# The third tile's x loaded ahead of the second half of the key weights, two copies moved between engines, one normalisation put later

## The chip, the cores and the metric

One core of a Trainium2 chip runs the whole program. The metric is the device time of one execution in microseconds; less is better. The kernel before takes 1095.43 us, the median of three runs (1094.91 to 1096.3).

## The reference, cut to what matters

x is 2048 tokens of 576 features. A gate g = sigmoid(x · gate_w) mixes a linear-attention block and a channel MLP:

```python
q, k, v = split(x @ wqkv)                    # 32 heads of 18
pq, pk  = phi(q), phi(k)                     # phi(t) = where(t > 0, t + 1, exp(t)) + 1e-6
kv, z   = einsum(pk, v), pk.sum(tokens)      # per head
a = ((pq @ kv) / (pq . z + 1e-6)) @ wo
b = gelu(layernorm(x) @ w1 + b1) @ w2 + b2   # w1: 576 x 4608, w2: 4608 x 576
out = g * a + (1 - g) * b
```

## The kernel before, in words

Work on tokens goes by tiles of 128, sixteen in all, in the order of a list ORDER; `first` is its first three (called tile 0, 1 and 2 below). Every matrix is multiplied in float32 by splitting both factors into a high part (float32r, what TensorE multiplies at speed) and a low part (the rest), and by summing high·high, low·high and high·low. A split is thus always two steps: a copy that rounds to the high part, and a subtraction on VectorE (DVE) that gives the low part. Nearly everything is recorded through a small helper (line 120), so that profile lines read L120 and are told apart by the names of their tiles.

Each engine does its instructions in the order in which the program writes them; nothing reorders them. The second half of the program (the MLP) is written in an order that a planner computes; the change does not touch it.

Names at the start. `t` is the raw x of a tile, loaded transposed in three DMAs on the queue of SyncE (SP): the main part from `in_xm` (256 KB) and two from `in_xe` (32 KB each). `s` is a raw half of a weight matrix: the main part from `in_wm` (576 KB) and two from `in_we` (72 KB each). There are four halves: KEY 0, KEY 1, QUERY 0, QUERY 1. The main part of KEY 0 comes in three pieces on ScalarE's (ACT's) queue. `y` holds the split x and the split weights. `split_x` and `split_w` make them: the copy on ACT, the low part on DVE. KEY 1 is 128x1450 (two more columns per row block than QUERY 0's 128x1440, for the sums that the gate and the layer norm need).

`first_keys(n, half)` is 14 matmuls of TensorE (PE): tile n times a half of the key weights. Its order takes the high·high products first, then low x · high weights, and those with the weights' low part from the tenth on. `both_phi(n)` applies phi to both halves of tile n's keys: for each half two instructions on ACT (`e<-ps`, `e<-e`) and one on DVE (`k<-ps,e`), then two short ones for the sums of x (`gsum`, `nmean`). The tile `e` has two buffers, so that the third `e<-ps` waits until DVE has read the first. `first_queries(n, half)` are the same 14 matmuls with the query weights; their results alternate between two PSUM banks, 6 and 7, so that tile 2's may only start when phi of tile 0's has been read from bank 6 by DVE (`accs<-ps,e`).

Loads: every DMA that SP or ACT issues takes the next of eight semaphores in turn, and waits until the DMA eight places earlier has landed (the `DMAHW` waits below).

Some 190 us later the attention's output matrix is made. `project_values(t)`, t = 0 to 4, computes one of five row blocks of `wp` on PE (12 matmuls; 6 for the last) into one of two pairs of PSUM banks in turn (banks 6 and 7 for t = 0, 2, 4; banks 4 and 5 for t = 1, 3); ACT copies the high part out (`wp<-ps`), DVE subtracts for the low part (`wp<-ps,wp`), and then the pair is free. `normalize(i, (1,))` multiplies tile i's phi(q) by its reciprocal denominator on DVE (`accs<-accs,den`); `tail_q(i)` copies its last 64 columns on ACT (`tail<-accs`). `transpose_q(i)` turns tile i on PE (`ps<-accs`, `ps<-accs,tail`) and splits it (`qt`). Between `transpose_q(0)` and `transpose_q(1)` PE projects the last tile's queries (28 matmuls, `ps<-y`) into banks 4 and 5.

Of the kernel before, what the change touches and what calls it, by code (L numbers as in the profile page):

```python
# [11 lines left out]
AF = mybir.ActivationFunctionType  # L12
# [81 lines left out]
def raw(ap):  # L94
    return ap.bitcast(F32)


def halves(ap):
    return ap.rearrange("p (a n) -> p a n", a=2)


def heads(ap):
    return ap.rearrange("p (h d) -> p h d", d=DH)


def half_cols(half):
    return slice(half * HALF, (half + 1) * HALF)
# [19 lines left out]
def tile_gated_mix(ctx: ExitStack, tc: tile.TileContext, x, xm, xe, wm, we, wvm, wve, wo, um, ue, w2, b1, b2, gw, out):  # L127
    nc = tc.nc
    pe, act, dve, pool = (InOrder(tc, e) for e in (nc.tensor, nc.scalar, nc.vector, nc.gpsimd))
# [9 lines left out]
    def two_of(ring):  # L139
        n = next(ring)  # L140
        return ps[:, n:n + 2]
# [4 lines left out]
    def load_twice(dst, src, by=sp):  # L146
        for half in range(2):
            by.dma_start(dst[half * 64:(half + 1) * 64], src)
# [48 lines left out]
    QUERY, KEY = range(2)  # L197
# [25 lines left out]
    def load_w(part, half, pieces=((0, 5),), by=sp):  # L223
        if (part, half) not in wraw:
            wraw[part, half] = wsp.tile([P, 5, HALF + 2], F32, name="s", tag="s")
        s = wraw[part, half]
        main = wm[part * 2 + half].rearrange("p (t n) -> p t n", t=4)
        tail = we[part * 2 + half]
        for t0, t1 in pieces:
            if t0 < 4:  # L230
                by.dma_start(s[:, t0:min(t1, 4), :HALF], main[:, t0:min(t1, 4)])
            if t1 == 5:
                load_twice(s[:, 4, :HALF], tail, by)

    def split_w(part, half, by=dve, pieces=((0, 5),)):
        w = W[part, half]
        s = wraw[part, half][:, :, :w.shape[2]]
        for t0, t1 in pieces:
            act.activation(w[:, t0:t1], s[:, t0:t1], AF.Copy)
            by.tensor_tensor(out=w[:, 5 + t0:5 + t1], in0=s[:, t0:t1], in1=raw(w[:, t0:t1]), op=OP.subtract)  # L240

    def load_x(i):
        xraw[i] = yt.tile([P, 5, P], F32, name="t")
        sp.dma_start(xraw[i][:, 0:4], xm[i].rearrange("p (t n) -> p t n", t=4))
        load_twice(xraw[i][:, 4], xe[i])

    def split_x(i, pieces=((0, 5),)):
        if i not in xs:
            xs[i] = x_places[PLACE[i] % X_RING]
        to, src = xs[i], xraw[i]  # L250
        for t0, t1 in pieces:
            act.activation(to[:, t0:t1], src[:, t0:t1], AF.Copy)
            if t0 < 4:
                dve.tensor_sub(to[:, 5:9], src[:, 0:4], raw(to[:, 0:4]))
            if t1 == 5:
                dve.scalar_tensor_tensor(to[:, 4], raw(to[:, 4]), low_half[:, 0:1], src[:, 4], op0=OP.mult, op1=OP.add)
# [12 lines left out]
    def project(i, part, half, order=BY_ROWS, n=None, between={}):  # L269
        w = W[part, half]  # L270
        p = banks[i, part, half] = ps[:, next(halves_in) if n is None else n]
        for m, (a, b) in enumerate(order):
            pe.matmul(p[:, :w.shape[2]], xs[i][:, a, :], w[:, b], start=(m == 0), stop=(m == len(order) - 1))
            if m in between:
                between[m]()
# [16 lines left out]
    def keys_phi(i, half):  # L292
        if half == 0:
            K[i] = kp.tile([P, D], F32, name="k")
        phi(K[i], i, KEY, half, (lambda: None, lambda: sums_of_x(i))[half])
# [152 lines left out]
    def load_y(sup, m):  # L448
# [3 lines left out]
    first = ORDER[:FIRST]  # L452
# [5 lines left out]
    act.activation(tiny, ones[:, 0:1], AF.Exp)  # L458
    load_w(KEY, 0, ((4, 5),), act)
    load_x(first[1])  # L460
    load_w(KEY, 1)
    load_x(first[2])
    load_w(QUERY, 0)
    load_xn(first[0])
    load_w(QUERY, 1)
# [4 lines left out]
                       base=0, channel_multiplier=1)  # L470
    pool.affine_select(blocks, blocks, pattern=[[DH, 7], [0, DH]], compare_op=OP.is_ge, fill=0.0,
                       base=DH - 1, channel_multiplier=-1)
    split_x(first[0], ((0, 4),))
    split_w(KEY, 0, pieces=((0, 1), (1, 2)))
    split_x(first[0], ((4, 5),))
    split_w(KEY, 0, pieces=((2, 4), (4, 5)))

    def first_keys(n, half, between={}):
        project(first[n], KEY, half, HI_FIRST, 3 * half + n, between)
# [4 lines left out]
    def both_phi(n):  # L484
        for half in range(2):
            keys_phi(first[n], half)
# [12 lines left out]

    first_keys(0, 0, {0: lambda: warm(1), 1: lambda: warm(1), 2: lambda: warm(1), 3: turn_gate})  # L500
    split_x(first[1])
    first_keys(1, 0)
    dve.tensor_copy(wraw[KEY, 1][:, :, HALF:HALF + 1], column[:, :, None])
    dve.memset(wraw[KEY, 1][:, :, HALF + 1:HALF + 2], 1.0)
    split_w(KEY, 1)
    split_x(first[2])
    load_x(ORDER[3])
    first_keys(0, 1)
    first_keys(1, 1)
    both_phi(0)  # L510
    split_w(QUERY, 0)
    first_keys(2, 0)
    first_keys(2, 1)
    both_phi(1)
    keys_split(first[0])
# [82 lines left out]
    for n in range(FIRST, NT):  # L598
        i, before = ORDER[n], ORDER[n - 1]
# [72 lines left out]
    def normalize(i, parts=(0, 1)):  # L672
        if 0 in parts:
            dens[i] = small.tile([P, H], F32, name="den")
        den = dens[i]
        if 0 in parts:
            dve.tensor_reduce(out=den, in_=heads(qz[i]), op=OP.add, axis=AX.X)
            dve.tensor_tensor(out=den, in0=den, in1=den0, op=OP.add)
            dve.reciprocal(den, den)
        if 1 in parts:  # L680
            dve.scalar_tensor_tensor(heads(acc[i]), heads(acc[i]), EPS_PHI, den[:, :, None].to_broadcast([P, H, DH]),
                                     op0=OP.add, op1=OP.mult)

    def tail_q(i):
        tails[i] = small.tile([P, P], F32, name="tail")
        act.activation(halves(tails[i]), acc[i][:, None, 4 * P:D].to_broadcast([P, 2, 64]), AF.Copy)
# [56 lines left out]
    def project_values(t):  # L743

        pw = two_of(w_pairs)
        own = [(n, j) for n, (to, j) in enumerate(PIECES) if to == t]
        for half in range(2):
            parts = [(kv_parts[a][:, n], wo_parts[b][:, j]) for a, b in TERMS for n, j in own]
            for m, (a, b) in enumerate(parts):
                pe.matmul(pw[:, half, :HALF], a, b[:, half_cols(half)], start=m == 0, stop=m == len(parts) - 1)  # L750
        p = pw[:, :, :HALF]
        act.activation(halves(wp[:, t]), p, AF.Copy)
        dve.tensor_tensor(out=halves(wp[:, 5 + t]), in0=p, in1=halves(raw(wp[:, t])), op=OP.subtract)
# [19 lines left out]
    normalize(1, (0,))  # L773
    project_values(1)
    project_values(2)
    normalize(1, (1,))
    tail_q(1)
    project_values(3)
    project_values(4)
    normalize(2, (0,))  # L780
    transpose_q(0)
    normalize(2, (1,))
# [861 lines left out]
```

## Time and profile before

| | |
|---|---|
| median of three runs | 1095.43 us (1094.91 to 1096.3) |
| the profiled execution, its time | 1096.17 us |
| the profiled execution, its span | 1094.5 us |
| PE busy | 1086.3 us, 99% of the span |
| DVE, ACT, POOL busy | 922.4, 691.3, 236.2 us |
| granted PE clock | full in all forty slices |

PE is the matmuls, PEld the weight loads that overlap them; SPq is SP's queue, that is the instructions that issue DMAs. In a timeline a row is: start in us, duration in us, engine, line, operation, what it writes <- what it reads, shape, how many; in brackets the idle time before it and what ended it. In the chain of waits (the work that ended last, followed back from the end) a row is: start, duration, what.

### The profile page before, as it was taken

Reading aid. Unit: us, or ns where it says so; the run is one execution under the profiler, and the core shown is the slowest. Engines: PE = TensorE matmul, PEld = TensorE weight load, DVE = VectorE, ACT = ScalarE, POOL = GpSimd, SP = SyncE. Lnnn points to the kernel's source line nnn. Section 1 sums busy time; section 2 is a strip of 40 time slices with the busy share of each in tenths; the row PEclk is TensorE's granted clock in tenths of the full one; section 3 lists DMA queues with packets and bytes.
Section 4 is the critical chain, followed back from the end, with each engine's and each line's share of the span. In section 5 each row is a group of like instructions: output and inputs, shape, how many; then the busy total and the mean of one; then the engine's idle time right before and its main releaser. Section 6 shows DMA issues by size and latency. Waiting matters only on the chain.

```text
span 1094.5 us, 18650 instructions
## 1 busy us (share of the span) xinstructions
PE 1086.3 (99%) x6712; PEld 996.6 (91%) x6712; DVE 922.4 (84%) x1558; ACT 691.3 (63%) x1235; POOL 236.2 (22%) x232
## 2 busy tenths in 40 slices
PE   9999999999999999999999999999999999999998
PEld 8999999999898889988889988989899999999898
DVE  4568786896799999899999997988887888878888
ACT  6677766454667887777877876455555555455552
POOL 2111113431123232332111202121122211221110
PEclk9999999999999999999999999999999999999999
DMA  6466772745745665764556559574444445444432
GB/s 179 135 87 190 172 218 101 278 178 191 249 156 188 196 203 185 239 209 169 194 184 220 191 197 396 170 252 118 135 148 118 130 119 148 131 122 118 133 102 87
DMA packets 109006, 189.72 MB, mean 173 GB/s; under 512 B 8940, under 2 KB 68604, under 8 KB 104818
## 3 DMA queue, kind: packets, MB, share of 16 engines
q1 hardware_dynamic: 108002, 187.78, 53.7%
q8 instruction: 53, 0.87, 0.3%
q10 hardware_dynamic: 720, 0.74, 0.2%
q14 instruction: 39, 0.32, 0.1%
q0 software_dynamic: 192, 0.01, 0.0%
HBM read 121.70 MB, written 66.80 MB: 172 GB/s over the span
## 4 chain that ended last, share of the span: by engine, by line
PE 92%; DVE 3%; DMA 3%; ACT 1%; issue 0%; SPq 0%; ACTq 0%; DVEq 0%
PE ps L120 92%; DVE accs L120 1%; DMA accs<-moments 1%; DMA yd<-ystage 1%; DMA s<-in_wm 0%; DVE h L120 0%; DMA ystage<-late_acc 0%; DMA fresh<-in_ue 0%; DMA s<-in_we 0%; DVE wa L120 0%; DVE region L120 0%; DVE ystage L120 0%; DVE wb L120 0%; DVE fresh L120 0%; ACT u L120 0%
## 5 line engine op out<-in xcount | busy, mean ns | idle before, releaser
L120 PEld LDWEIGHTS ps<-region,h 128*128 128x128 f32 x3072 | 437.5, 188 | 30.2 <-ACT ps L120 4.7
L120 PE MATMUL ps<-region,h 128*128 128x288 f32 x3072 | 456.8, 295 | 0.8 <-DVE accs L120 0.7
L120 DVE TENSOR_TENSOR accs<-ps,accs 128x576 f32<-128x576 f32 x330 | 246.1, 753 | 60.7 <-PE ps L120 53.9
L120 PE MATMUL ps<-y,wa 128*128 128x512 f32 x1008 | 257.6, 392 | 0.0
L120 PEld LDWEIGHTS ps<-y,wa 128*128 128x128 f32 x1008 | 180.8, 188 | 30.5 <-ACT ps L120 0.2
L120 POOL TENSOR_TENSOR fresh<-fresh 128x288 f32<-128x288 f32 (+1 forms) x128 | 117.1, 918 | 409.5 <-DVE accs L120 144.5
L120 PE MATMUL ps<-y,wb 128*128 128x512 f32 x756 | 199.2, 393 | 0.4 <-ACT u L120 0.4
L120 DVE TENSOR_TENSOR h<-u,h 128x512 fp32r<-128x512 f32 x240 | 165.4, 702 | 8.7 <-ACT u L120 8.7
L120 PEld LDWEIGHTS ps<-y,wb 128*128 128x128 f32 x756 | 133.8, 188 | 21.1 <-ACT u L120 0.6
L120 PE MATMUL ps<-y 128*128 128x288 f32 (+2 forms) x950 | 133.9, 297 | 2.2 <-DVE wp L120 1.1
L120 PEld LDWEIGHTS ps<-y 128*128 128x128 f32 (+1 forms) x950 | 129.8, 188 | 4.4 <-DVE wp L120 1.8
L120 ACT ACTIVATE region<-fresh 128x576 fp32r<-128x576 f32 (+1 forms) x132 | 81.2, 625 | 73.9 <-PE ps L120 73.3
L120 ACT ACTIVATE ps<-ps 128x576 f32<-128x576 f32 (+1 forms) x127 | 78.6, 621 | 45.0 <-PE ps L120 21.5
L120 POOL TENSOR_TENSOR u<-u 128x512 f32<-128x512 f32 x44 | 57.1, 1298 | 193.2 <-DVE h L120 54.8
L120 DVE TENSOR_TENSOR region<-fresh,region 128x576 fp32r<-128x576 f32 (+1 forms) x132 | 94.3, 727 | 1.1 <-ACT region L120 1.1
L120 ACT ACTIVATE u<-ps 128x512 f32<-128x512 f32 x73 | 43.0, 589 | 68.2 <-PE ps L120 68.2
L120 ACT ACTIVATE h<-u 128x512 fp32r<-128x512 f32 x128 | 73.4, 621 | 9.9 <-DVE u L120 5.5
L120 ACT ACTIVATE h<-u,b1s 128x512 fp32r<-128x512 f32 x73 | 52.6, 722 | 42.2 <-DVE u L120 42.1
L120 PE MATMUL ps<-wp,qt 128*128 128x288 f32 x448 | 63.0, 297 | 0.0
L120 DVE TENSOR_TENSOR u<-ps,u 128x512 f32<-128x512 f32 x74 | 50.4, 683 | 13.6 <-PE ps L120 12.7
L120 PEld LDWEIGHTS ps<-wp,qt 128*128 128x128 f32 x448 | 59.8, 188 | 0.0
L120 DVE TENSOR_TENSOR u<-u 128x512 f32<-128x512 f32 x84 | 58.0, 691 | 1.7 <-POOL u L120 1.1
(139 smaller groups left out, 1044.8 us busy)
## 6 DMA issues: line engine op xcount, KB each, us to landing
w1d<-wa SPq DMA_DIRECT2D x17, 1280.0 KB
wa<-w1d SPq DMA_DIRECT2D x68, 320.0 KB
fresh<-in_w SPq DMA_DIRECT2D x70, 288.0 KB
y<-yd SPq DMA_DIRECT2D x14, 1280.0 KB
w1d<-wb SPq DMA_DIRECT2D x17, 960.0 KB
wb<-w1d SPq DMA_DIRECT2D x51, 320.0 KB
yd<-ystage SPq DMA_DIRECT2D x28, 320.0 KB
fresh<-in_um SPq DMA_DIRECT2D x64, 128.0 KB
```

Of the source, the lines that this page charges most:

```text
L120: self.last = self.tc.keep_in_program_order(op(*args, **kwargs))
```

## The change

Three edits at two places.

1. At the start SP issues the three loads of tile 2's x ahead of those of KEY 1. To go with it, tile 2's x is split, and multiplied with KEY 0, before KEY 1 is split; and QUERY 0 is split before phi of tile 0's keys.
2. The high part of tile 0's x (its main part, 128x512) is copied by DVE and no longer by ACT.
3. Around 200 us, `normalize(1, (1,))` moves behind `project_values(3)`, and `tail_q(1)` behind `project_values(4)`.

```diff
-    def split_x(i, pieces=((0, 5),)):
+    def split_x(i, pieces=((0, 5),), on_dve=False):
...
-            act.activation(to[:, t0:t1], src[:, t0:t1], AF.Copy)
+            if on_dve:
+                dve.tensor_copy(to[:, t0:t1], src[:, t0:t1])
+            else:
+                act.activation(to[:, t0:t1], src[:, t0:t1], AF.Copy)
...
     load_x(first[1])
+    load_x(first[2])
     load_w(KEY, 1)
-    load_x(first[2])
     load_w(QUERY, 0)
...
-    split_x(first[0], ((0, 4),))
+    split_x(first[0], ((0, 4),), on_dve=True)
...
     first_keys(1, 0)
+    split_x(first[2])
+    first_keys(2, 0)
     dve.tensor_copy(wraw[KEY, 1][:, :, HALF:HALF + 1], column[:, :, None])
     dve.memset(wraw[KEY, 1][:, :, HALF + 1:HALF + 2], 1.0)
     split_w(KEY, 1)
-    split_x(first[2])
     load_x(ORDER[3])
     first_keys(0, 1)
     first_keys(1, 1)
+    split_w(QUERY, 0)
     both_phi(0)
-    split_w(QUERY, 0)
-    first_keys(2, 0)
     first_keys(2, 1)
...
     project_values(1)
     project_values(2)
+    project_values(3)
     normalize(1, (1,))
+    project_values(4)
     tail_q(1)
-    project_values(3)
-    project_values(4)
     normalize(2, (0,))
```

SP's queue at the start, before (-) and after (+); the rows ahead of these are tile 0's and tile 1's x:

```order
-L120 DMA s<-in_wm 128x4x288 [waits DMAHW2_49]
-L120 DMA s<-in_we 64x288 [waits DMAHW4_49]
-L120 DMA s<-in_we 64x288 [waits DMAHW5_49]
-L120 DMA t<-in_xm 128x512 [waits DMAHW6_49]
-L120 DMA t<-in_xe 64x128 [waits DMAHW7_49]
-L120 DMA t<-in_xe 64x128 [waits DMAHW0_49]
+L120 DMA t<-in_xm 128x512 [waits DMAHW2_49]
+L120 DMA t<-in_xe 64x128 [waits DMAHW4_49]
+L120 DMA t<-in_xe 64x128 [waits DMAHW5_49]
+L120 DMA s<-in_wm 128x4x288 [waits DMAHW6_49]
+L120 DMA s<-in_we 64x288 [waits DMAHW7_49]
+L120 DMA s<-in_we 64x288 [waits DMAHW0_49]
```

The six loads have changed places three by three; each place keeps its semaphore, so KEY 1's main load now stands in the place that waits for `DMAHW6`, tile 1's main part.

ACT at the start, before (-) and after (+): 128x640 is a tile's x, 128x1450 is KEY 1, 128x1440 is QUERY 0, `e` is phi of keys.

```order
-L120 ACTIVATE y<-s 128x1450 [waits DMAHW4_49,DMAHW5_49,DMAHW2_49,DVE_49]
-L120 ACTIVATE y<-t 128x640 [waits DMAHW7_49,DMAHW6_49,DMAHW0_49]
-L120 ACTIVATE e<-ps 128x288 [waits PE_49]
-L120 ACTIVATE e<-e 128x288 [waits Activation_49]
-L120 ACTIVATE e<-ps 128x288 [waits PE_49]
-L120 ACTIVATE e<-e 128x288 [waits Activation_49]
-L120 ACTIVATE gsum<-ps 128x1
-L120 ACTIVATE nmean<-ps 128x1
+L120 ACTIVATE y<-t 128x640 [waits DMAHW5_49,DMAHW4_49,DMAHW2_49]
+L120 ACTIVATE y<-s 128x1450 [waits DMAHW6_49,DMAHW7_49,DMAHW0_49,DVE_49]
 L120 ACTIVATE y<-s 128x1440 [waits DMAHW3_49,DMAHW2_49,DMAHW1_49]
```

Tile 2's x now goes ahead of KEY 1, and the six instructions of phi of tile 0, which stood between KEY 1 and QUERY 0, stand behind QUERY 0 (their added rows follow directly).

DVE around 200 us, before (-) and after (+): `wp` is a row block's low part, `accs<-accs,den` the normalisation of tile 1.

```order
 L120 RECIPROCAL den<-den 128x32 [waits DVE_49]
-L120 TENSOR_TENSOR wp<-ps,wp 128x576 [waits Activation_49] x2
+L120 TENSOR_TENSOR wp<-ps,wp 128x576 [waits Activation_49] x3
 L120 SCALAR_TENSOR_TENSOR accs<-accs,den 128x576 [waits DVE_49]
-L120 TENSOR_TENSOR wp<-ps,wp 128x576 [waits Activation_49] x2
+L120 TENSOR_TENSOR wp<-ps,wp 128x576 [waits Activation_49]
 L120 TENSOR_REDUCE den<-qz 128x32 [waits Pool_49]
```

The fourth row block's low part now stands ahead of the normalisation. On ACT, likewise, the copies of the fourth and fifth row blocks stand ahead of `tail<-accs`, which waits for that normalisation.

## Prediction

> **What bounds the kernel now.** I read the page first, then the chain of waits whole, at the start and around 200 us, and then the timelines of the engines there.
>
> ```profile
> span 1094.5 us, 18650 instructions
> PE 1086.3 (99%) x6712; PEld 996.6 (91%) x6712; DVE 922.4 (84%) x1558; ACT 691.3 (63%) x1235; POOL 236.2 (22%) x232
> ...
> 14.48 182.82 PE ps L120 x1229
> 201.67 320.14 PE ps L120 x1996
> ```
>
> PE is idle for 1094.5 - 1086.3 = 8.2 us in all, and the chain is PE alone from 14.48 to 197.30 and from 201.67 to 521.8. So whatever PE gains or loses at the two places of the change is kept, one for one, and no more than a few microseconds are to be had. A measurement of this kernel tells about 0.2%, 2.2 us, from no change.
>
> The two breaks of the chain are where the change works. The first, as the chain has it:
>
> ```profile
> 1.74 4.98 DMA s<-in_wm
> ...
> 7.25 3.94 DMA s<-in_we
> ...
> 11.30 1.43 ACT y L120
> ...
> 12.75 1.68 DVE y L120
> ```
>
> KEY 1's last small load, issued at 7.25, lands at 11.19; ACT copies the high parts from 11.30, DVE makes the low parts from 12.75, and PE goes on at 14.48. The second:
>
> ```profile
> 197.32 0.66 ACT wp L120
> ...
> 198.01 0.76 DVE wp L120
> 198.76 1.19 DVE accs L120
> ...
> 199.98 0.31 ACT tail L120
> 200.29 0.55 ACT wp L120
> ...
> 200.86 0.77 DVE wp L120
> ```
>
> The fourth row block's copy (ACT 200.29, DVE 200.86) stands behind the third's, the normalisation and the tail, and PE waits for it until 201.67.
>
> **Part 3, around 200 us.** PE's weight loads:
>
> ```profile
> 195.43 1.62 PEld L120 LDWEIGHTS ps<-y 126*128 126x128 f32 x12 [0.17 <-DVE wp L120]
> 197.31 2.43 PEld L120 LDWEIGHTS ps<-y 126*128 126x128 f32 x18 [0.26 <-DVE wp L120]
> 201.67 3.75 PEld L120 LDWEIGHTS ps<-y 128*128 128x128 f32 x28 [1.38 <-DVE wp L120]
> ```
>
> The third row block begins at 195.43 and ACT copies it at 197.32, 1.89 later; the fourth begins at 197.31, so its copy can start at 199.20, if nothing stands ahead of it. After the change nothing does. DVE follows 0.69 after ACT (197.32 to 198.01), takes 0.76, and PE hears 0.04 later (200.86 + 0.77 to 201.67): 200.69 instead of 201.67, a gain of 0.98 of the 1.38 us idle. The bounds are narrow: the 28 matmuls can't start before the transposes of tile 0 end, so the gain is at most 1.38, and at least nothing. What moves back: the normalisation ends near 202 instead of 199.95. Its next reader is the transposition of tile 1, which PE reaches at 200.69 + 3.75 = 204.4, more than 2 us later. The tail's copy, now ahead of tile 0's `qt` on ACT, pushes that by less than 1 us, and PE reads `qt` only behind the transposition of tile 1. The fifth row block's low part goes behind the normalisation and stays near 202, where it was. Taken: -0.98.
>
> **Part 2, tile 0's copy on DVE.**
>
> ```profile
> 6.01 0.69 DVE L120 TENSOR_TENSOR y<-t,y 128x512 fp32r<-128x512 f32 x1 [4.62 <-ACT y L120]
> 6.75 0.67 ACT L120 ACTIVATE y<-s 128x576 fp32r<-128x576 f32 x1
> ```
>
> The trace has no such copy on DVE; the subtraction of the same shape, 0.69, bounds it above, 0 below. ACT is freed of one copy, but its third weight piece can't start earlier than 6.72 (1.74 + 4.98 in the chain above, the landing) and starts at 6.75 now. PE reaches that piece's products at the same time, and anyway waits at 12.77 for KEY 1 (below). Taken: 0, hidden by the load; were that cover gone, it would gain at most the 0.7 of a copy.
>
> **Part 1, the loads.** Two quantities decide: A, when ACT starts on KEY 1 (11.30 before), and S, when it starts on QUERY 0 (16.34 before). SP's queue now:
>
> ```profile
> 4.69 0.74 SPq L120 DMA_DIRECT2D s<-in_wm  x1
> 6.73 1.12 SPq L120 DMA_DIRECT2D s<-in_we  x2
> 7.90 0.58 SPq L120 DMA_DIRECT2D t<-in_xm  x1
> 8.52 1.11 SPq L120 DMA_DIRECT2D t<-in_xe  x2
> 9.68 0.60 SPq L120 DMA_DIRECT2D s<-in_wm  x1
> ```
>
> The first two rows are KEY 1, the next two tile 2's x, the last QUERY 0's main load. SP waited until 6.73 for a semaphore of KEY 0, so the places stay when the loads are swapped: KEY 1's main load moves from 4.69 to 7.90, its small loads from 6.73 to 8.52, the last one of them from 7.25 to about 9.07. That load took 3.94 from issue to landing; at 9.07 it lands at 13.0, and A is 13.1.
>
> ```profile
> core 0: us, PE busy (x) PEld busy (x) DVE busy (x) ACT busy (x) POOL busy (x), PEclk, DMA share, GB/s
> 12.00:14.00 2.00, 1.24 (x10) 1.23 (x9) 1.25 (x1) 1.97 (x4) 0.00 (x0) 1.00 1.03 292
> 14.00:16.20 2.20, 1.97 (x15) 1.73 (x15) 1.65 (x4) 0.84 (x3) 0.00 (x0) 1.00 1.05 368
> ```
>
> Bounds for A: tile 2's 320 KB at 368 GB/s put in front is 0.9, so 12.2 at best; QUERY 0, main load issued at 9.68 and ACT at it at 16.34, took 6.66, so 7.90 + 6.66 = 14.6 at worst. I take 13.1. For S: the same bytes lie ahead of QUERY 0 as before and its issue keeps its place, so 16.3 stays the value; best is 12.2 plus its 720 KB at 368 GB/s, 14.2, and worst 14.6 plus 720 KB at 292 GB/s, 17.1.
>
> PE has 14 more matmuls (tile 2 with KEY 0) to do while it waits:
>
> ```profile
> 8.56 3.45 PE L120 MATMUL ps<-y 128*128 128x288 f32 x24
> 12.77 1.24 PEld L120 LDWEIGHTS ps<-y 128*128 128x128 f32 x9 [0.99 <-ACT y L120]
> 14.47 11.91 PEld L120 LDWEIGHTS ps<-y 128*128 128x128 f32 x89 [0.47 <-DVE y L120]
> ```
>
> A matmul takes 11.91 / 89 = 0.134. The 89 are five of tile 0's keys and six groups of 14, of which tile 2's first queries are the last; they thus start at 14.47 + 75 x 0.134 = 24.5. After, PE goes on 3.18 after A (11.30 to 14.48, the same chain of ACT and DVE) with 61 left: A + 3.18 + 8.16 = A + 11.34. At A = 13.1 that is 24.44: the 1.87 us of filled waiting and the 1.8 us of later weights cancel.
>
> But ACT's order has changed, and there the change has its price. Phi of tile 0, done while QUERY 0 was on its way, now stands behind QUERY 0's copy, and with it the whole row of phis up to that of tile 0's queries, whose bank tile 2's queries need:
>
> ```profile
> 16.34 1.41 ACT L120 ACTIVATE y<-s 128x1440 fp32r<-128x1440 f32 x1
> 17.64 0.41 ACT L120 ACTIVATE e<-ps 128x288 f32<-128x288 f32 x1
> 18.43 0.39 ACT L120 ACTIVATE e<-ps 128x288 f32<-128x288 f32 x1
> 19.31 0.78 ACT L120 ACTIVATE ks<-k,eps 128x576 fp32r<-128x576 f32 x1
> 19.98 0.41 ACT L120 ACTIVATE e<-ps 128x288 f32<-128x288 f32 x1
> ...
> 22.94 0.41 ACT L120 ACTIVATE e<-ps 128x288 f32<-128x288 f32 x1 [0.86 <-PE ps L120]
> ...
> 17.78 1.66 DVE L120 TENSOR_TENSOR y<-s,y 128x1440 fp32r<-128x1440 f32 x1 [0.84 <-ACT y L120]
> 19.36 0.81 DVE L120 SCALAR_TENSOR_TENSOR k<-ps,e 128x288 f32<-128x288 f32 x2
> 23.86 0.46 DVE L120 SCALAR_TENSOR_TENSOR accs<-ps,e 128x288 f32<-128x288 f32 x1 [1.29 <-ACT e L120]
> ```
>
> From these rows, counted from S: DVE is through QUERY 0's low parts and starts tile 0's first `k` at S + 3.02 (16.34 to 19.36), and 0.46 later the buffer of `e` is free for tile 1 (S + 3.5; two halves of tile 0 on ACT are done by then). Tile 1: 0.79 for a half (17.64 to 18.43) and 0.88 for a half with its sums (18.43 to 19.31); `ks` 0.67 (19.31 to 19.98); tile 2: 0.79 + 0.88; then tile 0's queries, 0.92 on ACT until DVE starts (22.94 to 23.86) and 0.46 there: S + 3.5 + 1.67 + 0.67 + 1.67 + 1.38 = S + 8.9. Before, this chain ended at 24.32, barely ahead of PE's 24.5. Now tile 2's queries start at the later of A + 11.34 and S + 8.9; with 13.1 and 16.3 that is 25.2, a loss of 0.7. It ends between 23.5 (A 12.2, S 14.2), a gain of 1.0, and 26.0 (A 14.6, S 17.1), a loss of 1.5. Nothing behind gives it back: PE isn't idle again until 200 us.
>
> **Sum.** -0.98 + 0 + 0.7 = -0.25 us on the profiled execution's 1096.17, 1095.9. That execution was 0.7 above the median of the runs, 1095.43; so the median I forecast is 1095.2.
>
> **The rivals.** First, the loads run at their bounds: KEY 1 and QUERY 0, now one behind the other with no small x loads between them, move at the 368 GB/s of the fullest stretch, A = 12.2 and S = 14.2. Then both places gain, 0.98 + 0.97, and the time is 1093.5. Against it: the DMA queue needed until 16.34 for QUERY 0 at 292 to 368 GB/s. The Trainium skill, DMA: Bandwidth & Descriptors, section "Anatomy of one DMA", gives a load some 2 us plus its bytes at 436 GB/s. By that KEY 1 would be there at about 11.3 and QUERY 0 at about 13.4, and the time 1092.7; the same rule puts KEY 1's last small load of before at 9.4, where the trace has 11.19, so here it is queueing that counts. Chance 0.18 for this rival, 0.03 of it for the page's value.
>
> Second, slower: QUERY 0 lands late and ACT, which now holds all phis behind that one wait, stalls. The place is ACT's copy of 128x1440; each microsecond of S beyond 15.6 costs one. From S = 16.6 on, the loss exceeds the gain at 200 us; at S = 17.1 the time is 1096.0; beyond 0.2% it would be only from S = 18.8. For it: SP leaves the DMA queue short between 7.5 and 9, as now only two loads of 32 KB are issued there ahead of KEY 1. Chance 0.17, of which 0.04 beyond 0.2%.
>
> Third, part 3 gives nothing, if PE there waits for something else just as late. Against it: the chain runs through these instructions and no other. Time 1096.1; chance 0.04.
>
> **How the numbers follow.** My own case (A 12.6 to 13.9, S 15.4 to 16.6) has 0.61. The low end of the range, 1093.5, is the first rival's; the high end, 1096.9, is the start's worst case (1.5) with nothing gained at 200 us. Faster by over 0.2% (under 1093.2) needs the page's figures or a lucky median: 0.06; slower by over 0.2% (over 1097.6): 0.05; the rest, 0.89, is within 0.2%.
>
> **What would show it.** In the new profile: KEY 1's copy on ACT (128x1450) near 13.1 and QUERY 0's (128x1440) near 16.3 with ACT idle in front of it; PE idle near 25 ahead of 14 matmuls, released by DVE `accs`; PE's weight loads around 200 idle for some 0.4 instead of 1.38. I am wrong if QUERY 0 is there by 15.6, so that ACT's order costs nothing, or if something outside these 25 us moves.

## The result, and the profile after

The changed kernel takes 1096.87 us, the median of 14 runs (1095.7 to 1098.72), against 1095.45 us for the kernel before on the same chip (14 runs, 1094.34 to 1096.3). The ratio is 1.0016, 95% interval 1.0009 to 1.0023. It is slower by 1.4 us, where I forecast 0.25 us faster. The page has the same picture as before, PE at 99%:

```profile
span 1095.1 us, 18651 instructions
PE 1085.7 (99%) x6712; PEld 995.2 (91%) x6712; DVE 924.3 (84%) x1559; ACT 690.9 (63%) x1234; POOL 235.5 (22%) x232
```

The profiled execution took 1096.82 us, 0.65 more than the one of before; but the latter was 0.7 above its median, so the two traces show only half of the difference of the medians.

The chain of waits of the changed kernel, 0 to 33 us (start, duration, what), answers to the first break of the chain before:

```profile
9.17 4.03 DMA s<-in_we
...
13.28 1.42 ACT y L120
...
14.73 1.68 DVE y L120
...
16.45 8.46 PE ps L120 x61
24.91 0.40 ACT e L120
...
25.34 0.45 ACT e L120
...
25.81 0.47 DVE accs L120
...
26.33 6.69 PE ps L120 x39
```

KEY 1 is copied at 13.28 (forecast 13.1), PE goes on 3.17 later as worked out, and does its 61 matmuls. Then it waits, as forecast, for DVE's `accs`, the release of bank 6. (The chain puts PE ahead of ACT's 24.91, as the 61 matmuls end just then; an experiment below tells whether ACT waited for them.) But tile 2's queries start at 26.33, not at 25.2. PE's weight loads say the same, with the idle time in brackets; the last two rows are `wp`'s third row block and the 28 matmuls behind the fourth:

```profile
14.74 1.24 PEld L120 LDWEIGHTS ps<-y 128*128 128x128 f32 x9 [1.14 <-ACT y L120]
16.45 8.21 PEld L120 LDWEIGHTS ps<-y 128*128 128x128 f32 x61 [0.46 <-DVE y L120]
26.32 1.76 PEld L120 LDWEIGHTS ps<-y 128*128 128x128 f32 x13 [1.67 <-DVE accs L120]
...
197.60 1.61 PEld L120 LDWEIGHTS ps<-y 126*128 126x128 f32 x12 [0.16 <-DVE wp L120]
...
202.89 3.74 PEld L120 LDWEIGHTS ps<-y 128*128 128x128 f32 x28 [0.43 <-DVE wp L120]
```

The start lost 1.8 us; at 197.60 PE is 2.17 behind (195.43 before). Then it is idle for 0.43 instead of 1.38, 0.95 less. Where the missing 1.1 us of the start is lost is seen in the timelines of ACT, DVE and POOL of the changed kernel:

```profile
16.23 1.41 ACT L120 ACTIVATE y<-s 128x1440 fp32r<-128x1440 f32 x1 [1.54 <-DMA s<-in_we]
...
22.21 2.00 DVE L120 SCALAR_TENSOR_TENSOR ks<-k,ks 128x576 fp32r<-128x576 f32 x1 [0.21 <-ACT ks L120]
24.34 0.82 DVE L120 SCALAR_TENSOR_TENSOR k<-ps,e 128x288 f32<-128x288 f32 x2
25.81 0.46 DVE L120 SCALAR_TENSOR_TENSOR accs<-ps,e 128x288 f32<-128x288 f32 x1 [0.65 <-ACT e L120]
...
22.16 1.44 POOL L120 TENSOR_TENSOR pks<-pks,k 128x576 f32<-128x576 f32 x1 [1.37 <-DVE k L120]
```

and of the same two instructions before:

```profile
20.12 0.76 DVE L120 SCALAR_TENSOR_TENSOR ks<-k,ks 128x576 fp32r<-128x576 f32 x1
...
20.33 1.84 POOL L120 TENSOR_TENSOR pks<-pks,k 128x576 f32<-128x576 f32 x1 [2.66 <-DVE k L120]
```

`ks` is the low part of tile 0's phi(k), `pks` the running sum of phi(k) on GpSimd (POOL). Before, DVE began `ks` at 20.12, 0.2 ahead of GpSimd's sum: `ks` took 0.76, and the sum was long (1.84). After, phi of tile 1 is ready before ACT has made the high part of `ks`; GpSimd's sum begins at 22.16, 0.05 ahead of `ks`: the sum takes 1.44, and `ks` 2.00. It ends at 24.21, 0.61 after the sum (22.16 + 1.44 = 23.60). Behind it on DVE stand tile 2's `k` (24.34), which free `e` for ACT's phi of tile 0's queries (24.91), which frees bank 6.

What I could have seen: asked for this tile as a whole, the trace of before gives the spread of all its sixteen `ks` (durations in ns, least, median, most).

```profile
L120 DVE SCALAR_TENSOR_TENSOR ks<-k,ks x16: 749/1238/1348, 20.1 to 172.9; 128x576 fp32r<-128x576 f32 x16
```

The 0.76 us that I carried over was nearly the shortest of them, and the 2.00 of the changed kernel is longer than any.

### The profile page after: what moved, and what is told of

Same layout as the page of the kernel before. It is cut to its first block, busy times and chain, and to the rows that moved or that the text cites. A ratio compares the mean times of both kernels' runs of the same rounds, so it can differ in the third digit from the quotient of the medians.

```text
span 1095.1 us, 18651 instructions
## 1 busy us (share of the span) xinstructions
PE 1085.7 (99%) x6712; PEld 995.2 (91%) x6712; DVE 924.3 (84%) x1559; ACT 690.9 (63%) x1234; POOL 235.5 (22%) x232
## 4 chain that ended last, share of the span: by engine, by line
PE 92%; DMA 3%; DVE 2%; ACT 1%; issue 0%; SPq 0%; ACTq 0%; DVEq 0%
PE ps L120 92%; DMA moments<-mr 1%; DVE accs L120 1%; DMA accs<-in_xm 0%; DMA s<-in_wm 0%; DMA s<-in_we 0%; DMA ystage<-late_acc 0%; DMA xn<-in_x 0%; SPq L120 0%; DVE h L120 0%; ACT h L120 0%; ACT u L120 0%; DVE u L120 0%; ACT y L120 0%; ACT e L120 0%
```

## The experiments

The theory: whichever of the two engines starts first makes the other wait, and the new order of ACT and DVE puts GpSimd first. Its rivals: the loads alone make the start later; the new order alone does; or it is chance. Each kernel was run 11 times, one of them with a profile, against 33 runs of the kernel before on the same chip (medians 1094.79, 1094.8 and 1095.12 on the three chips). A and S are ACT's starts on KEY 1 and QUERY 0, as in the prediction.

**The two places apart.** The third edit alone, on the kernel before:

```diff
     project_values(2)
+    project_values(3)
     normalize(1, (1,))
+    project_values(4)
     tail_q(1)
-    project_values(3)
-    project_values(4)
```

> The kernel before with the third edit alone (tile 1's normalisation behind the fourth row block, its tail behind the fifth). Theory 1 (this edit does what the prediction said, and the loss is all at the start): PE idle ahead of the last tile's queries near 200 us falls from 1.38 to about 0.4, and the time falls by 0.9 to 1.0 us, to about 1094.5. Rival (the edit's gain is given back later, by DVE or the MLP): the idle falls, but the time stays within 0.3 us of before.

Measured: 1094.63 us, ratio 0.9999 [0.9990, 1.0008]. A second time, on another chip:

> The third edit alone on the kernel before, once more. Theory 1: PE's idle time near 200 us is 0.43 instead of 1.38 and the median is 0.6 to 1.0 below before; the first pair's 0.16 was noise of some 0.5. Rival (the gain is given back in the MLP, where PE waits for DVE and a load near 530 to 560 and 700 to 716 us): the idle is gone, but the median is again within 0.3 of before, and PE's idle between 520 and 720 us has grown by as much.

Measured: 1095.13 us, 1.0004 [0.9995, 1.0013]. In both traces PE is idle for 0.43 at the place. The medians, though, are 0.2 below and 0.3 above before, each uncertain by about 1 us: the 0.6 to 1.0 that were expected are not seen, and a smaller gain is not resolved. The traces speak against the rival, that the MLP gives the gain back. From the start of the last tile's query matmuls, behind the place, to the end of the span it is 892.41 us on the mean of the four traces without the edit (891.9 to 892.8) and 892.39 on that of the ten with it (891.2 to 893.2).

The rest, that is the changed kernel with the third edit taken back:

> The changed kernel without its third edit: the start alone. Theory 1: everything lost is lost at the start, so the time is 0.95 above the changed kernel, about 1097.8, 2.4 above before; tile 2's first queries start near 26.3 as in the changed kernel. Rival (the loss is somewhere behind): not more than 1.4 above before.

Measured: 1096.86 us, 1.0018 [1.0009, 1.0027]. So the start alone makes the loss. It is 2.1 us by the medians, where 2.4 was expected; the rival's 1.4 lies inside the interval too.

```profile
21.50 2.00 DVE L120 SCALAR_TENSOR_TENSOR ks<-k,ks 128x576 fp32r<-128x576 f32 x1 [0.21 <-ACT ks L120]
...
21.45 1.44 POOL L120 TENSOR_TENSOR pks<-pks,k 128x576 f32<-128x576 f32 x1 [1.37 <-DVE k L120]
...
25.61 1.90 PEld L120 LDWEIGHTS ps<-y 128*128 128x128 f32 x14 [1.30 <-DVE accs L120]
```

The loads landed earlier in this execution (A 12.95, S 15.52), yet GpSimd is again 0.05 ahead, and `ks` takes 2.00.

**GpSimd's sum held back.** The changed kernel, with one wait added on GpSimd:

```diff
+        ks_low[i] = dve.last.ins.name
         sum_keys(i)
+        if i == first[1]:
+            tc.add_manual_dep(pool.last.ins, ks_low[first[0]], ...)
```

> The changed kernel with one wait more: GpSimd's sum of tile 1's keys (pks) starts only when DVE has done the low part of tile 0's keys (ks). Theory A (DVE's ks took 2.00 us instead of 0.76 because GpSimd's sum began 0.05 us ahead of it and the two can't run together): ks takes 0.76 again, phi of tile 0's queries starts on ACT near 23.7 instead of 24.89, tile 2's first queries start near 25.2 instead of 26.32, and the time falls by about 1.1 against the changed kernel, to 1095.7. Rival B (ACT waited there for PE, as the profile's bracket says): nothing moves, tile 2's queries start at 26.3 and the time stays at 1096.9.

Measured: 1095.68 us, 1.0004 [0.9996, 1.0013], as expected.

```profile
22.48 0.76 DVE L120 SCALAR_TENSOR_TENSOR ks<-k,ks 128x576 fp32r<-128x576 f32 x1 [0.21 <-ACT ks L120]
...
23.39 2.95 POOL L120 TENSOR_TENSOR pks<-pks,k 128x576 f32<-128x576 f32 x2 [2.34 <-DVE ks L120]
...
17.30 10.05 PEld L120 LDWEIGHTS ps<-y 128*128 128x128 f32 x75 [0.46 <-DVE y L120]
```

`ks` is back at 0.76, and PE runs 75 matmuls (the 61 and tile 2's 14) without a stall on `accs`. The loads were late here (A 14.13), so tile 2's queries start at 17.30 + 61 x 0.134 = 25.5. ACT's phi of tile 0's queries starts at 24.01 here, well before the 61 matmuls end; so it was not PE that ACT waited for in the changed kernel. Once more, on a third chip:

> The kernel of pool_later once more: the changed kernel with GpSimd's sum of tile 1 waiting for tile 0's ks on VectorE. Theory: ks 0.76 and no stall of PE on VectorE ahead of tile 2's first queries; these start at A + 11.34 or S + 8.9, whichever is later, as in the first run (25.45 with A = 14.13); time 0.2 to 1.2 us under the changed kernel, by what the loads do. Rival (the first run's gain was chance): no difference from the changed kernel's 1096.2 to 1096.9.

Measured: 1096.33 us, 1.0009 [1.0000, 1.0018]; `ks` 0.76, A 14.13, S 17.01, queries at 25.96. The short stall on `accs` of 0.44 is that of a late QUERY 0 (S + 8.9 = 25.9).

The same by order alone, `ks` of tile 0 ahead of tile 1's phis:

```diff
     both_phi(0)
+    keys_split(first[0])
     first_keys(2, 1)
     both_phi(1)
-    keys_split(first[0])
```

> The changed kernel, with both copies of tile 0's keys (ks) moved ahead of tile 1's phis instead of behind them; GpSimd's sum of tile 1 then comes after ks by the order alone, with no wait added. Theory: ks takes 0.76 again, and tile 2's first queries start at the later of A + 11.34 and S + 8.9 (A and S: ScalarE's starts on KEY 1 and QUERY 0), between 24.4 and 25.5 depending on the loads, 0.9 to 1.9 earlier than in the changed kernel; the time is 0.9 to 1.9 under it and about that of before. Rival (the later phis alone cost the 1.8 us): tile 2's queries stay near 26, and the time is that of the changed kernel.

Measured: 1096.31 us, 1.0011 [1.0002, 1.0020]; `ks` 0.76, GpSimd's sum 2.3 later than it, A 13.75, S 16.28, queries at 25.65. That is 0.5 over the later of A + 11.34 and S + 8.9 (25.2): ACT now waits 0.85 for `k` ahead of `ks`. The stretch is gone in the trace. The time is not what was expected: 0.9 to 1.9 under the changed kernel was forecast, but the ratio is hardly below that kernel's, and the intervals overlap.

**GpSimd put first in the kernel before.** The opposite step, with the order of before otherwise kept:

```diff
+        if i == first[0]:
+            dve.tensor_copy(ks[:, 1, :HALF], k[:, :HALF])
         dve.scalar_tensor_tensor(ks[:, 1], k, EPS_PHI, raw(ks[:, 0]), ...)
```

> The kernel before, with one copy of 128x288 on VectorE (into a half of ks that ks itself then overwrites) put just ahead of the low part of tile 0's keys (ks). It delays ks by about 0.25 us, to behind the release of GpSimd's sum (20.33 in the trace of before). Theory (whoever of the two engines starts first makes the other wait): GpSimd's sum starts at 20.3 to 20.4 and takes 1.44, ks takes 2.00 instead of 0.76, and the chain to tile 2's first queries, which had 0.2 us to spare, ends 1.5 later: these start near 25.8, and the time is 1.2 to 1.4 us over before. Rival (ks was long in the changed kernel for another reason, such as its new neighbours on ScalarE): ks stays at 0.76, GpSimd's sum at 1.84, tile 2's queries start at 24.5 to 24.6, and the time is that of before within 0.2 us.

Measured: 1094.81 us, 0.9995 [0.9986, 1.0003].

```profile
20.13 0.30 DVE L120 CAST ks<-k 128x288 fp32r<-128x288 f32 x1
20.54 1.89 DVE L120 SCALAR_TENSOR_TENSOR ks<-k,ks 128x576 fp32r<-128x576 f32 x1
...
24.03 0.46 DVE L120 SCALAR_TENSOR_TENSOR accs<-ps,e 128x288 f32<-128x288 f32 x1 [0.65 <-ACT e L120]
...
20.37 1.44 POOL L120 TENSOR_TENSOR pks<-pks,k 128x576 f32<-128x576 f32 x1 [2.66 <-DVE k L120]
...
14.51 11.92 PEld L120 LDWEIGHTS ps<-y 128*128 128x128 f32 x89 [0.46 <-DVE y L120]
```

Half of the expectation held, half missed. The mechanism is shown: one copy of 0.30 us lets GpSimd's sum go first, and `ks` takes 1.89 instead of 0.76. The price is not: `accs` starts at 24.03 instead of 23.86, and PE's 89 matmuls run through. In the order of before DVE stood idle for 0.64 and 1.29 us between `ks` and `accs`, since ACT's phi there waited for PE; this idle time swallowed the 1.5. The two rows of before:

```profile
22.11 0.46 DVE L120 SCALAR_TENSOR_TENSOR k<-ps,e 128x288 f32<-128x288 f32 x1 [0.64 <-ACT nmean L120]
...
23.86 0.46 DVE L120 SCALAR_TENSOR_TENSOR accs<-ps,e 128x288 f32<-128x288 f32 x1 [1.29 <-ACT e L120]
```

So a long `ks` costs nothing in the order of before, and its whole 1.24 in the new order, where DVE has no idle time to give. Both are needed for this part of the loss: GpSimd ahead, and a chain without idle time.

**The loads and the order apart.** The changed kernel unaltered, for a second trace:

> The changed kernel, unaltered, on the chip of the three that follow, so that they can be compared with it. Theory A (start: KEY 1 on ACT at 13 to 14, then GpSimd's sum of tile 1's keys meets DVE's ks): ks takes 2.00 us, tile 2's first queries start A + 13 or later, 1.0 to 1.6 us slower than before. Rival (that stretched ks belonged to one execution): ks takes 0.76 here, and the time is within 0.6 of before.

Measured: 1096.21 us, 1.0012 [1.0003, 1.0021]; A 13.50, S 16.40, `ks` 1.99, queries at 26.49. The same with the loads in their old order:

```diff
-    load_x(first[2])
     load_w(KEY, 1)
+    load_x(first[2])
```

> The changed kernel with the loads alone in the old order (KEY 1, then tile 2's x), and the new order of the work on PE, ACT and DVE. Theory A (half of the loss is ACT's order: phis behind QUERY 0's copy): tile 2's x lands near 12.1 and holds KEY 1's copy on ACT until 12.8; QUERY 0's copy starts at 16.3 as before, and so tile 2's first queries start at 25.2, or 26.3 if GpSimd's sum meets ks, no earlier than in the changed kernel's chain; time 0 to 1.3 above before. Rival C (the late loads are all of the loss): with KEY 1's landing back at 11.2, tile 2's queries start before 24.5, and the time is 0.5 to 1.0 below before.

Measured: 1096.5 us, 1.0016 [1.0007, 1.0025].

```profile
12.03 0.74 ACT L120 ACTIVATE y<-t 128x640 fp32r<-128x640 f32 x1 [2.71 <-DMA t<-in_xe]
13.87 2.71 ACT L120 ACTIVATE y<-s 128x1450 fp32r<-128x1450 f32 x2 [1.11 <-DVE s L120]
...
12.80 0.69 DVE L120 TENSOR_TENSOR y<-t,y 128x512 fp32r<-128x512 f32 x1 [2.49 <-ACT y L120]
...
13.67 0.16 DVE L120 COPY s<-ps 128x5 f32<-128x5 f32 x1
...
21.61 2.00 DVE L120 SCALAR_TENSOR_TENSOR ks<-k,ks 128x576 fp32r<-128x576 f32 x1 [0.21 <-ACT ks L120]
...
25.73 1.90 PEld L120 LDWEIGHTS ps<-y 128*128 128x128 f32 x14 [0.47 <-DVE accs L120]
```

The new order of the work is enough for the loss. The run was meant to bring KEY 1 back to its old time and does not, so it does not price the late loads by themselves: rival C, with queries before 24.5, is not borne out, but its condition did not come about. What holds KEY 1's copy here is DVE: the last load of tile 2's x lands at 12.0, ACT copies it, DVE makes its low part from 12.80, and only behind that, in the new order, does DVE write KEY 1's two additional columns (`s<-ps` at 13.67), for which ACT waits. So A is 13.87, not the 12.8 that was expected, and as late as with the loads in the new order (12.95 to 14.13); the prediction has no term for this wait, though in the changed kernel itself it is a load that releases KEY 1's copy. And `ks` is 2.00 again.

Two kernels put phi of tile 0 back ahead of QUERY 0; the second also loads KEY 1's main part ahead of tile 2's x:

```diff
-    split_w(QUERY, 0)
     both_phi(0)
+    split_w(QUERY, 0)
```

and, in the second alone:

```diff
+    load_w(KEY, 1, ((0, 4),))
     load_x(first[2])
-    load_w(KEY, 1)
+    load_w(KEY, 1, ((4, 5),))
```

> The changed kernel with phi of tile 0's keys put back ahead of the split of QUERY 0. Theory A (ACT's order is the price): phi of tile 0 is done by 18.3, QUERY 0's copy starts near 18.3, and tile 2's first queries start near 25.0 if GpSimd's sum doesn't meet DVE's ks, near 26.2 if it does; the time is 1095.6 or 1096.7. Rival C (the late KEY 1 alone is the price): tile 2's queries stay near 26.3 whatever the order, and ACT's phis wait for PE.

Measured: 1094.99 us, 1.0006 [0.9997, 1.0015], the most scattered of all; four of its eleven executions took 1096.7 us or more.

> The changed kernel with KEY 1's main load first, then tile 2's three x loads, then KEY 1's two small loads, and with phi of tile 0's keys ahead of QUERY 0's split. Theory A (the main load's late issue and ACT's order are the two prices): KEY 1's small loads are issued from 8.5 on and land near 12.1, KEY 1's copy on ACT starts near 12.2 (13.28 changed, 11.30 before), tile 2's first queries start at 23.6 to 24.1 (24.5 before), and with the third edit's 0.95 the time is 1.0 to 1.8 below before. Rival (whatever is put ahead of KEY 1's last small load delays it as much as the change did): its copy starts at 13 or later and the time is that of the variant with phi first, within 0.5 of before.

Measured: 1095.63 us, 1.0005 [0.9996, 1.0014]. In both, `ks` (0.76) goes ahead of GpSimd's sum again; A is 14.06 and 13.99, and tile 2's queries start at 25.84 and 25.78 (25.0 was expected of the first, with QUERY 0's copy near 18.3; it started at 19.10). In the second, KEY 1's main part, issued at 4.81, landed at 10.73, and SP, which needs its semaphore for QUERY 0's small loads, stood still from 9.45 until then. There too ACT waits for DVE's columns behind tile 2's x, which lands at 12.1. So the second kernel's expectation missed: KEY 1 was to start near 12.2, and the time to be 1.0 to 1.8 below before; it is the rival's that came. Neither is shown to beat before.

**The kernel before again**, for the chance in its own trace:

> The kernel before, unaltered, for a second profiled execution and a measure of chance. Expected by all theories: a ratio of 1 within 0.1%. If the profiled execution used for the prediction was a slow one (it was 0.7 us over the median), this one has a span of 1093.5 to 1094, the same first 200 us within 0.2 us, and the difference lies after 530 us, where the other kernels' traces differ by chance too. If instead before is always as in its first profile, the span is 1094.5 again.

Measured: 1095.0 us, 0.9999 [0.9990, 1.0007].

```profile
span 1092.6 us, 18650 instructions
...
10.60 1.42 ACT L120 ACTIVATE y<-s 128x1450 fp32r<-128x1450 f32 x1 [1.11 <-DVE s L120]
...
11.84 13.85 PEld L120 LDWEIGHTS ps<-y 128*128 128x128 f32 x102
```

The expectation of equal first 200 us missed: KEY 1 came 0.7 earlier here, PE hardly waited for it, and 0.7 of the 1.9 us between the two spans arose at the start. Another 0.5 arose near 200 us, by the same meeting of two engines, and 0.4 near 710 us, where a load took 4.25 instead of 3.84. The rows at 200 us, of the first profile of before, of this one, and of the start alone, in that order; POOL adds two parts of `accs`, released by a load, and DVE normalises:

```profile
198.31 1.02 POOL L120 TENSOR_TENSOR accs<-accs 128x384 f32<-128x384 f32 x1 [0.75 <-DMA accs<-in_ue]
198.68 1.26 DVE L120 SCALAR_TENSOR_TENSOR accs<-accs,den 128x576 f32<-128x576 f32 x1
```

```profile
197.06 1.02 POOL L120 TENSOR_TENSOR accs<-accs 128x384 f32<-128x384 f32 x1 [0.23 <-DMA accs<-in_ue]
197.99 0.75 DVE L120 SCALAR_TENSOR_TENSOR accs<-accs,den 128x576 f32<-128x576 f32 x1
...
200.46 1.62 PEld L120 LDWEIGHTS ps<-y 128*128 128x128 f32 x12 [0.88 <-DVE wp L120]
```

```profile
199.17 1.03 POOL L120 TENSOR_TENSOR accs<-accs 128x384 f32<-128x384 f32 x1 [0.46 <-DMA accs<-in_ue]
199.83 0.98 DVE L120 SCALAR_TENSOR_TENSOR accs<-accs,den 128x576 f32<-128x576 f32 x1
...
202.54 3.74 PEld L120 LDWEIGHTS ps<-y 128*128 128x128 f32 x28 [1.11 <-DVE wp L120]
```

In the first profile GpSimd's addition was still running (until 199.33) when DVE's normalisation began, which then ended at 199.94, 0.61 later. In the second it was all but over, and the normalisation took 0.75. So the 1.38 us idle on which the prediction rested held 0.5 us of a meeting that occurs in some executions, as a load lands.

## Why the prediction was wrong, point by point

- **Part 2, 0:** held. DVE's copy took 0.43 at 3.97, and ACT's third weight piece started at 6.71 instead of 6.75. No run has this edit by itself.
- **Part 3, -0.98:** right against the profile it was made from (1.38 to 0.43), but mis-sized for the runs. Without the edit, PE was idle there for 1.38, 1.11, 0.88 and 0.87 (before, the start alone, before again, the copy of 0.30); the mean is 1.06, and the gain on the mean 0.63. I took the chain's `198.76 1.19 DVE accs` as the price of the work; 0.75 is its price without GpSimd beside it.
- **Part 1, A 13.1 and S 16.3:** S held, A was somewhat too early. A was 13.28 in the first trace, and 13.69 on the mean of seven executions with the new order of loads (12.95 to 14.13), inside the case's 12.6 to 13.9 on the mean though not in each; S was 16.32 on the mean of the six of them that have phi behind QUERY 0. The 0.6 by which A is late on the mean does not change the term, as S + 8.9 (25.2) is still the later one (13.69 + 11.34 is 25.0). The first rival's figures from the Trainium skill, DMA: Bandwidth & Descriptors, section "Anatomy of one DMA", are given there for DMAs that GpSimd issues, where SP issues these; by them KEY 1 would have been there at about 11.3, and none of the seven executions has A before 12.95.
- **Part 1, "with 13.1 and 16.3 that is 25.2, a loss of 0.7":** this is the step that failed. The chain of S + 8.9 took over `ks` as it lay in the old order, at 0.76 and hidden beside ACT's phi of tile 2. The table sets the formula against the executions that have this order; with GpSimd first, 1.24 (2.00 - 0.76) is added to the chain of S. The 1.24 is read from these traces, so the first three rows show that it closes the gap, not that it could be foreseen.

| execution | A | S | `ks` | later of A + 11.34, S + 8.9 (+ 1.24) | measured |
|---|---|---|---|---|---|
| changed kernel | 13.28 | 16.23 | 2.00 | 26.37 | 26.32 |
| the same again | 13.50 | 16.40 | 1.99 | 26.54 | 26.49 |
| start alone | 12.95 | 15.52 | 2.00 | 25.66 | 25.61 |
| sum held back | 14.13 | 16.50 | 0.76 | 25.47 | 25.5 |
| sum held back, again | 14.13 | 17.01 | 0.76 | 25.91 | 25.96 |

  The form of the term was right to 0.05 us in these five; what it lacked is one stretched instruction. With the loads in their old order it falls short by 0.4 us (13.87 and 15.19 give 25.33, measured 25.73), since ACT there waits 0.68 for PE in phi of tile 0, and with `ks` put first by 0.5, as told above. None of the three rivals was this one; the slower rival named a late QUERY 0, and QUERY 0 was on time. That 1096.87 is just inside the top of the range, 1096.9, is luck: this top was built of late loads and of no gain at 200 us.
- **The sum.** The forecast's terms add up to -0.28, not -0.25. PE reaches `wp`'s third row block at 195.43, 195.32, 195.26, 195.47 and 194.72 in five executions with the old start, and at 197.60, 197.63 and 196.58 in three with the new one and the long `ks`: 2.03 later on the mean. Of this, 1.24 is the stretch and 0.6 the rest of the start (forecast 0.7); some 0.2 arose between 28 and 195 us and was not traced further. With 0.63 gained near 200 us that makes +1.40, where the medians have +1.42. So close an agreement is luck, and the 0.63 rests on the traces alone, as told above: after 530 us the executions drift apart by up to 1 us either way, for reasons that I did not study.
- **Not shown:** that taking away the stretch makes the kernel faster by 1.2 us. The three runs that do so and change nothing else lie at 1.0004, 1.0009 and 1.0011, the changed kernel at 1.0016 and 1.0012; the direction agrees, but the intervals overlap. In the traces of those three A was later, too (13.75 to 14.13 against 12.95 to 13.50 in the three with the new loads and the long `ks`), so that PE reached `wp`'s third row block only 0.66 earlier on the mean (196.61 against 197.27). Over all versions of the start the order is clean: the four runs whose trace has the long `ks` are at 1.0012 to 1.0018, the five without it at 1.0004 to 1.0011, 0.9 us apart on the mean. But they differ in other edits as well, and each has only one execution traced. No version tried is shown to beat the kernel before; the third edit alone is the best of them in the traces (spans 1092.9 and 1092.7), but before again had 1092.6.

## What to carry to other kernels

When an edit changes which of two engines comes first, don't carry the duration of an instruction over from its old place: ask the trace for all instructions of the same form, and if their spread is wide (here 749 to 1348 ns), find what ran on GpSimd beside the long ones and which started first. A long instruction then costs only where its engine has no idle time left behind it, so count that idle time in the new order. And a place that one profile shows idle for 1.4 us may owe a third of it to a load that landed at a bad moment; with an effect of a microsecond a second profile of the kernel before is worth more than another decimal of the first.

## What the runs showed of the hardware

A DVE instruction with two inputs in SBUF that meets a GpSimd instruction which began ahead of it ends about 0.61 us after GpSimd's ends, whenever it began, unless its own 0.75 last longer. That is `ks` at 24.21 against 23.60 in the changed kernel, 22.43 against 21.81 with the copy of 0.30, 23.50 against 22.89 with the start alone; and the normalisation at 199.94 against 199.33, and at 200.81 against 200.20. In the first 240 us of each of the fourteen traces the `ks` and the normalisations that met a GpSimd instruction so, some twenty in a trace, end 0.60 to 0.63 after it; one, at 197.99, met only the last 0.09 us of it and took its own 0.75. The other way round, GpSimd's sum took 1.84 instead of 1.44 and ended 1.29 after `ks`. The Trainium skill, SBUF — State Buffer, section "Who interferes with whom", says so: a DVE instruction with two SBUF inputs contends with a GpSimd instruction that reads SBUF, and "Issue order, not op shape, decides who blocks." The traces here agree, with the numbers above. I had not applied it, since in the profile that I read both instructions stood side by side, with the short one on DVE.

The landing of KEY 1's last small load behind the same queue varied by 1.2 us over seven executions of five kernels with the same order of loads, on several chips (A from 12.95 to 14.13), which is as much as most terms of the sum.
